# Queries and keys of twelve attention groups: a dense load, one split and a trip through DRAM in place of a threefold load and four splits

## Chip, core and metric

The kernel runs on one core of a Trainium2 chip. The metric is the device time of one execution in microseconds (us): the median over runs. Beside it stands one profiled execution, whose trace gives every row below. Its span is the time from its first to its last instruction.

## What is computed

Three layers in a row, all in float32: a gated linear attention over 4 batches, 8 heads, 768 positions and head dimension 40 (a recurrence with a forget gate, an input gate and an output gate), then a first feed-forward layer (320 to 768 to 320, the maximum of three projections), then a second one (320 to 2048 to 320, with h * relu6(h + 3) / 6).

```python
for t in range(S):                                   # attention
    m_new = np.maximum(f_gate[:, :, t] + m, i_gate[:, :, t])
    f_stab = np.exp(f_gate[:, :, t] + m - m_new); i_stab = np.exp(i_gate[:, :, t] - m_new); m = m_new
    C = f_stab * C + i_stab * outer(vt, kt);  n = f_stab * n + i_stab * kt
    y[:, :, t] = sigmoid(o_gate) * (C @ qt) / max(|n . qt|, 1)
h = np.maximum(np.maximum(x @ w1, x @ w2), x @ w3);  x = h @ w_out
h = x @ w_in;  out = (h * np.clip(h + 3, 0, 6) / 6) @ w_out
```

## The kernel before

The attention is cut into chunks of 128 positions: 6 chunks times 4 batches make 24 groups, numbered 0 to 23 in the code (the first one is group 0), each with all 8 heads. A group loads its queries and keys (`lq`, line 443), its keys, values and output gates in rows of positions (`lk`, line 454) and, from group 4 on, the forget factors (`fl`, line 504). VectorE scans the decays (`scan`, line 510); TensorE makes the scores (`sc`, line 538), the part from the earlier state (`inter`, line 566), the values' product (`pv`, line 608), the change of the state (`dc`) and a transpose of the result (`tr`); GpSimd, VectorE and ScalarE do what lies between. The first feed-forward layer (`f_in`, `f_out`, lines 789 and 822; its matmuls are those of lines 300, 833 and 835) works on blocks of groups, `BLK1` = 2, 2, 4, 4, 4, 4, 4, and is interleaved with the attention of later groups. The second layer follows (lines 953 to 1050); its start overlaps with the end of the first.

TensorE multiplies float32 in one pass when its operands are rounded (type F32R). Groups from 8 (`GF`) on therefore use a high part and a low part, and three products stacked along 120 partitions: rows 0 to 39 hold high times high, rows 40 to 79 and 80 to 119 one high and one low part. Before the change each of the groups 8 to 23 gets there so: `lq` loads q and k each three times, with six transfers of 40 x 1024 elements, into two `raw` buffers of 120 partitions; then, for q and k (`a`) and both halves of the heads (`z`), ScalarE writes the part to be taken away (`hm`, line 471: a copy scaled by 0 or 1 of each partition, from `lows`), and VectorE (q) or GpSimd (k) subtracts it (`ls`, line 476) into `qs`, the operand of the scores. `raw` and `qs` have two buffers, `sp` has one.

The order of all of this first part is made by a planner, not by hand: `Plan.add` (line 143) takes each step with its engine, an assumed duration, a priority and the tags that it reads and writes; `Plan.order` (line 160) simulates five in-order engines (SP issues the transfers), a clock of TensorE and the free buffers of `BUFS`, and takes whatever can start first, the lower priority number deciding ties. `MOVED` is a list of offsets to single steps' priorities. The result is a fixed order on each engine; on the chip each engine takes its instructions strictly in that order. The steps of the weights of the first layer (`weights`, line 747) load each tile into a ring of four buffers `wr` of 128 x 3072 bytes (`load_f64`, line 262); the second layer's weights use the same ring later (line 965).

Of the kernel before, what the change touches and what calls it, by code (L numbers as in the profile page):

```python
# [9 lines left out]
F32 = mybir.dt.float32  # L10
F32R = mybir.dt.float32r
# [5 lines left out]
ALU = mybir.AluOpType  # L17
# [3 lines left out]
B, H, S, D = 4, 8, 768, 40  # L21
L = 128
NC_ = S // L
G = B * NC_
# [3 lines left out]
K1, K2 = FF1 // 128, FF2 // 128  # L28
DP = 42
NBC, GF, G3 = 4, 8, 8  # L30
WC, OC = 384, 320
BLK1 = [2, 2, 4, 4, 4, 4, 4]
JOIN, LAG1 = 4, 3
# [2 lines left out]
AHEAD, WP0, WPR = 6, 500, 100  # L36
GP, NSG = 1055, 4
GPB, GGB = 3, 4
WLP, QLP = 800, 4000
PE_, PM, PC = 0, 2 * 10**6, 3 * 10**6  # L40

MOVED = {
# [20 lines left out]
}  # L63
NM1, NM2 = max(BLK1) * L, max(BLK2) * L

BUFS = dict(
    qs=2, raw=2, sp=1, kvo=2, kvg=2, fd=2, vt=2, vw=2, nm=2, rr=2, y=2, sg=2, ct=1, cn=B, ch=1, cs=B,
    pr=1, vr=1, wr=4, wa=2, x1=2, m=2, hh=3, x2=1, pa=3, h=2, acc0=1, acc1=1, acc2=1,
)
# [6 lines left out]
def top(x):  # L76
    return x.bitcast(BF16).rearrange("p h (t two) -> p h t two", two=2)[..., 1]


def low(x):  # L80
    return x.bitcast(BF16).rearrange("p h (t two) -> p h t two", two=2)[..., 0]
# [160 lines left out]
def body(tc, ctx, qk0, qkf, kvo, ig, fg, w1, w2, out):  # L242
    nc = tc.nc
# [4 lines left out]
    stg = ctx.enter_context(pool("stg"))  # L248
    dram = ctx.enter_context(pool("dram", 1, space=DRAM))
    psh = ctx.enter_context(pool("psh", 1, space=PSUM))  # L250
    psa = ctx.enter_context(pool("psa", 3, space=PSUM))

    f0_d = dram.tile([NC_ - 1, BH, L], F32, name="f0_d")
    x2_d = [dram.tile([128, 3, n * L], F32, name=f"x2_d{j}") for j, n in enumerate(BLK2)]

    def prio(p):
# [49 lines left out]
    with ExitStack() as c1:  # L306
# [5 lines left out]
        def sb(tag, g, shape, dt=F32, p=None):  # L312
            return (p or at).tile(shape, dt, tag=tag, name=f"{tag}{g}", bufs=BUFS[tag])
# [8 lines left out]
        lows = cs1.tile([120, 2], F32, name="lows")  # L322
        dL = cs1.tile([128, NC_ - 1, BH // 2], F32, name="dL")
        P = Plan()
# [3 lines left out]
        def gates(gp1, c0, c1_, pr):  # L328
# [96 lines left out]
            if c0:  # L425
# [2 lines left out]
                P.add("PE", 250, pr + 1500, dl1, r=[("dls",), ("own",)], w=[("pa", "dlp")])  # L428
                P.add("ACT", 230, pr + 1500, dl2, r=[("pa", "dlp")], w=[("dL",)])

        def attention(g):
            c, b = divmod(g, B)
            pr = 1000 * g
            j = next(j for j, (a, e) in enumerate(SP1) if a <= g < e)
            gi = g - SP1[j][0]
            s = T[g] = {}
            keep = c < NC_ - 1
            per_head = lambda x: x.unsqueeze(2).to_broadcast([128, H, DP])
            QS, FD, KVO = [("qs", g, a, z) for z in range(2) for a in range(2)], [("fd", g, a) for a in range(2)], ("kvg" if g < 2 else "kvo", g)
# [3 lines left out]
            def lq(a=0):  # L443
                if g < GF:
                    s["qs"] = sb("qs", g, [128, 2, 4, L])
                    for r in range(2):
                        nc.sync.dma_start(s["qs"][64 * r:64 * r + D], qk0[g][r])
                else:

                    s["raw", a] = q = sb("raw", f"{g}_{a}", [120, H, L])  # L450
                    for r in range(3):
                        nc.sync.dma_start(q[r * D:r * D + D].rearrange("p h t -> p (h t)"), qkf[g - GF, :, a])
# [8 lines left out]

            if g < GF:
                P.add("SP", 680, pr - 2100, lq, w=QS, size=4 * 40 * 2048)
            else:
                for a in range(2):
                    P.add("SP", 1100, pr - QLP + 400 * a, lambda a=a: lq(a), r=[("pv", g - AHEAD)], w=[("raw", (g, a))], size=120 * 4096)
            P.add("SP", 360, pr - 2000, lk, w=[KVO], size=4 * 128 * 976)

            if g >= GF:

                def hm(a, z):
                    s["sp", a, z] = sb("sp", f"{g}_{a}{z}", [120, 4, L], F32R)
                    x = s["raw", a][:, 4 * z:4 * z + 4]
                    nc.scalar.activation(s["sp", a, z], x, AF.Copy, scale=lows[:, a:a + 1])  # L474

                def ls(a, z):
                    if "qs" not in s:
                        s["qs"] = sb("qs", g, [120, 2, H, L], F32R)
                    x = slice(4 * z, 4 * z + 4)
                    eng = nc.gpsimd if a else nc.vector  # L480
                    eng.tensor_tensor(out=s["qs"][:, a, x], in0=s["raw", a][:, x], in1=s["sp", a, z].bitcast(F32), op=ALU.subtract)  # L481

                for z in range(2):
                    for a in range(2):
                        SPL, Q = ("sp", (g, a, z)), ("qs", g, a, z)
                        P.add("ACT", 600, pr - QLP + 1000 + z, lambda a=a, z=z: hm(a, z), r=[("raw", (g, a)), ("lows",)], w=[SPL])
                        P.add("POOL" if a else "DVE", 1220 if a else 600, pr - QLP + 1000 + z, lambda a=a, z=z: ls(a, z), r=[("raw", (g, a)), SPL], w=[Q])

            def fds():
                s["fd"] = sb("fd", g, [128, H, L])  # L490
# [106 lines left out]
            def pr0(a):  # L597
                if "pr" not in s:
                    s["pr"] = sb("pr", g, [128, H, L])
                x = slice(a * 4, a * 4 + 4)  # L600
                nc.vector.tensor_tensor(out=s["pr"][:, x], in0=s["fd"][:, x], in1=top(s["fd"])[:, x], op=ALU.subtract)

            def pr1(a):
                x = slice(a * 4, a * 4 + 4)
                eng = nc.vector if a else nc.gpsimd
                eng.tensor_tensor(out=low(s["pr"])[:, x], in0=s["pr"][:, x], in1=top(s["pr"])[:, x], op=ALU.subtract)
# [15 lines left out]
            if g >= G3:  # L622
                VR, PR = ("vr", g), [("pr", g, a) for a in range(2)]
                P.add("POOL", 800, pr + 31, vr0, r=[("vt", g)], w=[VR])
                P.add("POOL", 800, pr + 32, vr1, w=[VR])
                for a in range(2):
                    P.add("DVE", 830, pr + 33 + a, lambda a=a: pr0(a), r=[FD[a]], w=[PR[a]])
                    P.add("DVE" if a else "POOL", 1000 if a else 1310, pr + 36 + a, lambda a=a: pr1(a), w=[PR[a]])
                more = [VR, *PR]
            P.add("PE", 1290 if more else 1890, pr + 40, pv, r=[*FD, ("vt", g), *more], w=[PV, ("pv", g)], wait=300)  # L630

# [247 lines left out]
        def ids():  # L879
# [16 lines left out]
                out=sel, in0=ident[0:2 * BH, 0:BH], in1=ident[0:2 * BH, BH:2 * BH], op=ALU.add  # L896
# [187 lines left out]
def build(arrays):  # L1084
    nc = bacc.Bacc("TRN2", target_bir_lowering=False, num_devices=1)
    args = {
        n: nc.dram_tensor(f"in_{n}", a.shape, mybir.dt.from_np(a.dtype), kind="ExternalInput").ap()
        for n, a in arrays.items()
    }
    out = nc.dram_tensor("out_0", (B * S, DM), F32, kind="ExternalOutput").ap()  # L1090
    with tile.TileContext(nc, schedule_with_timeline_sim=True) as tc, ExitStack() as ctx:
        body(tc, ctx, out=out, **args)
    return nc
# [9 lines left out]
```

## Time and profile before

| | us |
|---|---|
| median of three runs | 798.19 |
| the three runs | 796.95, 799.6, 798.19 |
| the profiled execution | 794.38 |
| its span | 792.7 |
| TensorE busy in the span | 758.5 (96%) |
| GpSimd busy | 462.4 (58%) |
| VectorE busy | 437.4 (55%) |
| ScalarE busy | 353.3 (45%) |

PE is TensorE, PEld its weight loads, DVE VectorE, ACT ScalarE, POOL GpSimd, SP the engine that issues the transfers; a "q" behind the name means the sequencer of that engine. Busy shares are means over stages with different limits, so the rows below go by stretches of the span. A matmul's end is modelled, and a busy TensorE can still hold small gaps.

### The profile page before, as it was taken

What the parts mean: (1) busy time and instruction counts of PE and PEld (TensorE: products, weight loads), DVE (VectorE), ACT (ScalarE), POOL (GpSimd) and SP (SyncE); (2) the same over time, 40 slices, a digit from 0 to 9 for tenths busy, and PEclk for the clock granted to TensorE, in tenths of its full rate; (3) what the DMA queues carried; (4) which work ended last, traced back from release to release, by engine and by line L of the source; (5) the groups of instructions that cost most, each with busy time, mean ns of one, the idle gap of its engine ahead of it and who ended that gap; (6) DMA issues with size and microseconds to landing.
All of it is one profiled execution on the core that took longest, in us unless ns stands there. A gap on an engine that the chain in (4) does not pass through costs nothing.

```text
span 792.7 us, 13185 instructions
## 1 busy us (share of the span) xinstructions
PE 758.5 (96%) x5081; PEld 653.8 (82%) x5081; DVE 437.4 (55%) x652; ACT 353.3 (45%) x677; POOL 462.4 (58%) x420
## 2 busy tenths in 40 slices
PE   8899899899899999999899999999999999999997
PEld 5599898777777878778688888898999889898986
DVE  6868979889889888886414665313122113121210
ACT  4667633333334335332415887534433334433432
POOL 4568878998898887675512556544335334343332
PEclk9569989999999999999999999999999999999999
DMA  8578645344344435420502652100100000000000
GB/s 268 172 198 275 217 130 172 108 133 142 118 138 162 154 116 165 115 70 34 153 17 70 189 174 73 67 1 6 62 1 1 33 1 1 34 1 1 34 0 34
DMA packets 28654, 76.05 MB, mean 96 GB/s; under 512 B 3920, under 2 KB 9136, under 8 KB 28592
## 3 DMA queue, kind: packets, MB, share of 16 engines
q1 hardware_dynamic: 28592, 75.22, 30.1%
q8 instruction: 40, 0.66, 0.3%
q14 instruction: 22, 0.18, 0.1%
HBM read 65.54 MB, written 7.95 MB: 93 GB/s over the span
## 4 chain that ended last, share of the span: by engine, by line
PE 59%; DVE 13%; POOL 12%; ACT 7%; issue 5%; DMA 3%; SPq 0%; POOLq 0%; DVEq 0%; ACTq 0%
PE pi L300 20%; PE h L300 12%; PE po L1025 6%; PE po L1024 6%; PE po L1026 6%; POOL qs L481 3%; PE acc L833 3%; DVE fd L514 2%; DVE t L283 2%; POOL hh L817 2%; DVE qs L481 2%; POOL cs L730 1%; ACT a L271 1%; PE sc L544 1%; POOL y L655 1%
## 5 line engine op out<-in xcount | busy, mean ns | idle before, releaser
L1010 POOL TENSOR_TENSOR gg<-r,gg 128x512 fp32r<-128x512 f32 x96 | 125.7, 1318 | 183.2 <-ACT gg L1009 173.1
L300 PE MATMUL h<-x,w 128*128 128x512 f32 (+1 forms) x1008 | 227.2, 374 | 5.4 <-ACT m L801 4.2
L300 PEld LDWEIGHTS h<-x,w 128*128 128x128 f32 x1008 | 172.7, 195 | 36.3 <-ACT m L801 6.3
L300 PE MATMUL pi<-xs,w 128*128 128x512 f32 x768 | 193.5, 395 | 2.5 <-ACT w L969 1.9
L1007 DVE SCALAR_TENSOR_TENSOR r<-r,pi 128x512 f32<-128x512 f32 x96 | 64.3, 687 | 229.3 <-ACT r L1006 229.0
L300 PEld LDWEIGHTS pi<-xs,w 128*128 128x128 f32 x768 | 140.7, 188 | 31.0 <-ACT w L969 2.6
L1006 ACT ACTIVATE r<-pi,b 128x512 f32<-128x512 f32 x96 | 63.9, 686 | 133.8 <-PE pi L300 133.2
L1024 PE MATMUL po<-w,gg 128*128 128x320 f32 x384 | 118.2, 310 | 0.6 <-ACT x L861 0.4
L1025 PE MATMUL po<-w,gg 128*128 128x320 f32 x384 | 117.9, 309 | 0.0
L1026 PE MATMUL po<-w,gg 128*128 128x320 f32 x384 | 111.1, 309 | 0.0
L817 POOL TENSOR_TENSOR hh<-m,hh 128x512 fp32r<-128x512 f32 (+1 forms) x42 | 56.6, 1347 | 39.1 <-ACT hh L813 39.0
L1024 PEld LDWEIGHTS po<-w,gg 128*128 128x128 f32 x384 | 72.1, 188 | 4.8 <-ACT x L861 0.7
L1009 ACT CAST gg<-r 128x512 fp32r<-128x512 f32 x96 | 58.9, 621 | 36.5 <-DVE r L1007 34.4
L1025 PEld LDWEIGHTS po<-w,gg 128*128 128x128 f32 x384 | 72.1, 188 | 3.1
L474 ACT ACTIVATE sp<-raw,lows 120x512 fp32r<-120x512 f32 x64 | 46.3, 724 | 62.7 <-POOL qs L481 35.2
L833 PE MATMUL acc<-hh,w 128*128 128x512 f32 (+1 forms) x252 | 74.1, 374 | 0.0
L803 DVE TENSOR_TENSOR m<-h,m 128x512 f32<-128x512 f32 (+1 forms) x84 | 50.7, 603 | 42.3 <-PE h L300 36.5
L1026 PEld LDWEIGHTS po<-w,gg 128*128 128x128 f32 x384 | 70.4, 188 | 0.8
L514 DVE TENSOR_TENSOR_SCAN fd<-fd,ident 128x512 f32<-128x512 f32 x40 | 66.1, 1661 | 2.2 <-DMA fd<-f_d 2.2
L290 POOL TENSOR_TENSOR w<-t,w 128x384 fp32r<-128x384 f32 (+2 forms) x46 | 46.3, 1015 | 26.8 <-ACT w L768 16.8
L481 POOL TENSOR_TENSOR qs<-raw,sp 120x512 fp32r<-120x512 f32 x32 | 49.1, 1534 | 12.9 <-ACT sp L474 10.9
L813 ACT CAST hh<-m 128x512 fp32r<-128x512 f32 (+1 forms) x42 | 23.4, 558 | 70.8 <-PE acc L833 66.0
(109 smaller groups left out, 1082.4 us busy)
## 6 DMA issues: line engine op xcount, KB each, us to landing
raw<-in_qkf SPq DMA_DIRECT2D x96, 160.0 KB
raw<-in_w SPq DMA_DIRECT2D x34, 384.0 KB
kvo<-in_kvo SPq DMA_DIRECT2D x22, 488.0 KB
fd<-f_d SPq DMA_DIRECT2D x20, 512.0 KB
raw<-in_w SPq DMA_DIRECT2D x22, 320.0 KB
out<-ob SPq DMA_DIRECT2D x24, 160.0 KB
xr<-x_d SPq DMA_DIRECT2D x6, 512.0 KB
qs<-in_qk SPq DMA_DIRECT2D x16, 160.0 KB
```

What stands on the lines that cost most here:

```text
L300: nc.tensor.matmul(ps, wt[:, a:a + 128], x[:, r], start=n == 0, stop=n == len(order) - 1)
L481: eng.tensor_tensor(out=s["qs"][:, a, x], in0=s["raw", a][:, x], in1=s["sp", a, z].bitcast(F32), op=ALU.subtract)
L514: nc.vector.tensor_tensor_scan(out=half, data0=s.get(("bc", a), half), data1=ident4.rearrange("p h t -> p (h t)"), initial=0.0, op0=ALU.mu ...
L817: nc.gpsimd.tensor_tensor(out=t[:, 1], in0=T["m", j, k], in1=t[:, 0].bitcast(F32), op=ALU.subtract)
L833: nc.tensor.matmul(acc[a], wo[:, a * 128:128 + a * 128], h, start=first, stop=last)
L1006: nc.scalar.activation(r, ps, AF.Relu, bias=b3)
L1007: nc.vector.scalar_tensor_tensor(out=r, in0=r, scalar=6.0, in1=ps, op0=ALU.min, op1=ALU.mult)
L1009: nc.scalar.copy(gg[:, 0], r)
L1010: nc.gpsimd.tensor_tensor(out=gg[:, 1], in0=r, in1=gg[:, 0].bitcast(F32), op=ALU.subtract)
L1024: nc.tensor.matmul(po[t], hi, wo[:, 0:320], start=first, stop=False)
L1025: nc.tensor.matmul(po[t], hi, wo[:, 320:640], start=False, stop=False)
L1026: nc.tensor.matmul(po[t], lo, wo[:, 0:320], start=False, stop=last)
```

## The change

Groups 8 to 11 stay as they were. Groups 12 (`GH`) to 23 get their operand in another way. One transfer brings q and k once, cut densely into 128 partitions of 640 elements, into a buffer of the ring `wr`. ScalarE copies all of it, rounded, to a second buffer of the ring (the high part); GpSimd subtracts that from the first into a third (the low part). Two transfers write both parts to a DRAM buffer of the group, and five transfers read from there into the 120 partitions of `qs`. The planner's assumed durations of the old split and of two VectorE steps of the values' product are raised, and `MOVED` is another list, so the order of the whole first part is new. Nothing else is changed.

```diff
+GH = 12
+QF = 2 * D * H * L // 128
...
 MOVED = {
...
+    qs_d = [dram.tile([2, D, 2, H * L], F32, name=f"qs_d{g}") for g in range(GH, G)]
...
+        flat = lambda x: x.rearrange("d a n -> (d a n)").rearrange("(p f) -> p f", f=QF)
...
+                elif g >= GH:
+                    s["raw"] = stg.tile([128, QF], F32, tag="wr", name=f"qraw{g}", bufs=BUFS["wr"])
+                    nc.sync.dma_start(s["raw"], flat(qkf[g - GF]))
...
+            elif g >= GH:
+                P.add("SP", 380, pr - 4000, lq, r=[("pv", g - AHEAD)], w=[("wr", (100 + g, 2))], size=4 * 128 * QF)
...
+            if g >= GH:
+                d = qs_d[g - GH]
+                def part(n):
+                    s["sp", n] = stg.tile([128, QF], F32R, tag="wr", name=f"q{n}{g}", bufs=BUFS["wr"])
+                    return s["sp", n]
+                def sq():
+                    nc.scalar.copy(part(0), s["raw"])
+                def sl():
+                    nc.gpsimd.tensor_tensor(out=part(1), in0=s["raw"], in1=s["sp", 0].bitcast(F32), op=ALU.subtract)
+                def sw(n):
+                    nc.sync.dma_start(flat(d[n]), s["sp", n].bitcast(F32))
+                def sr():
+                    s["qs"] = q = sb("qs", g, [120, 2, H, L], F32R)
+                    q = q.bitcast(F32).rearrange("p a h t -> p a (h t)")
+                    nc.sync.dma_start(q[0:D], d[0])
+                    for r, (zq, zk) in enumerate(((0, 1), (1, 0)), 1):
+                        nc.sync.dma_start(q[r * D:r * D + D, 0], d[zq, :, 0])
+                        nc.sync.dma_start(q[r * D:r * D + D, 1], d[zk, :, 1])
+                QR, QP = ("wr", (100 + g, 2)), [("wr", (100 + g, n)) for n in range(2)]
+                P.add("ACT", 760, pr - 3000, sq, r=[QR], w=[QP[0]])
+                P.add("POOL", 1650, pr - 3000, sl, r=[QR, QP[0]], w=[QP[1]])
+                for n in range(2):
+                    P.add("SP", 360, pr - 3000 + n, lambda n=n: sw(n), r=[QP[n]], w=[("qd", g, n)], size=4 * 128 * QF)
+                P.add("SP", 1720, pr - 2500, sr, r=[("qd", g, 0), ("qd", g, 1)], w=QS, size=120 * 8192)
+            elif g >= GF:
...
-                        P.add("ACT", 600, pr - QLP + 1000 + z, lambda a=a, z=z: hm(a, z), r=[("raw", (g, a)), ("lows",)], w=[SPL])
-                        P.add("POOL" if a else "DVE", 1220 if a else 600, pr - QLP + 1000 + z, lambda a=a, z=z: ls(a, z), r=[("raw", (g, a)), SPL], w=[Q])
+                        P.add("ACT", 720, pr - QLP + 1000 + z, lambda a=a, z=z: hm(a, z), r=[("raw", (g, a)), ("lows",)], w=[SPL])
+                        P.add("POOL" if a else "DVE", 1320 if a else 850, pr - QLP + 1000 + z, lambda a=a, z=z: ls(a, z), r=[("raw", (g, a)), SPL], w=[Q])
...
-                    P.add("DVE", 830, pr + 33 + a, lambda a=a: pr0(a), r=[FD[a]], w=[PR[a]])
-                    P.add("DVE" if a else "POOL", 1000 if a else 1310, pr + 36 + a, lambda a=a: pr1(a), w=[PR[a]])
+                    P.add("DVE", 980, pr + 33 + a, lambda a=a: pr0(a), r=[FD[a]], w=[PR[a]])
+                    P.add("DVE" if a else "POOL", 1100 if a else 1310, pr + 36 + a, lambda a=a: pr1(a), w=[PR[a]])
```

## Rows read from the trace of the kernel before

**Rows 1.** Scores of line 544 from 170 to 360 us: durations, first and last start.

```profile
L544 PE MATMUL sc<-qs x96: 223/275/331, 176.3 to 356.0; 120*128 120x128 f32 x96
```

**Rows 2.** Stretches: length, each engine's busy time (instructions), clock, DMA share, GB/s.

```profile
core 0: us, PE busy (x) PEld busy (x) DVE busy (x) ACT busy (x) POOL busy (x), PEclk, DMA share, GB/s
0.00:120.00 120.00, 110.48 (x893) 95.32 (x894) 93.23 (x168) 70.62 (x161) 83.16 (x102) 0.84 0.68 210
120.00:170.00 50.00, 45.39 (x413) 38.49 (x413) 43.65 (x64) 17.27 (x34) 45.00 (x43) 0.97 0.43 136
170.00:360.00 190.00, 179.41 (x1451) 147.22 (x1450) 167.63 (x234) 74.55 (x138) 155.48 (x142) 1.00 0.41 129
360.00:400.00 40.00, 37.74 (x251) 30.44 (x250) 18.44 (x31) 12.77 (x22) 19.32 (x15) 1.00 0.33 101
400.00:520.00 120.00, 118.03 (x596) 101.36 (x596) 58.04 (x81) 73.75 (x151) 57.18 (x44) 1.00 0.29 95
520.00:760.00 240.00, 240.00 (x1328) 216.04 (x1327) 51.76 (x69) 93.91 (x154) 93.29 (x69) 1.00 0.04 15
```

**Rows 3.** TensorE's waits from 170 to 360 us: total, times, longest, in us.

```profile
PE sc L544 <- POOL qs L481: 5.8, 4, 2.0
PE h L300 <- ACT m L801: 1.8, 3, 0.7
PE dc L694 <- DVE x L675: 0.6, 1, 0.6
PE in L575 <- DVE qs L481: 0.6, 1, 0.6
PE tr L664 <- POOL y L655: 0.6, 1, 0.6
PE sc L544 <- DVE qs L481: 0.5, 1, 0.5
```

**Rows 4.** Groups by shape, 170 to 360 us: busy us, mean ns, idle before.

```profile
L481 POOL TENSOR_TENSOR qs<-raw,sp 120x512 fp32r<-120x512 f32 x23 | 36.8, 1602 | 9.2 <-ACT sp L474 7.5 <-issue 1.4
L474 ACT ACTIVATE sp<-raw,lows 120x512 fp32r<-120x512 f32 x46 | 33.3, 724 | 45.9 <-POOL qs L481 23.3 <-DVE qs L481 14.0 <-DMA raw<-in_qkf 7.7
L817 POOL TENSOR_TENSOR hh<-m,hh 128x512 fp32r<-128x512 f32 x18 | 26.8, 1487 | 9.2 <-ACT hh L813 9.2
L481 DVE TENSOR_TENSOR qs<-raw,sp 120x512 fp32r<-120x512 f32 x24 | 21.2, 884 | 6.3 <-ACT sp L474 6.1
L813 ACT CAST hh<-m 128x512 fp32r<-128x512 f32 x18 | 11.2, 620 | 33.1 <-PE acc L833 32.5 <-DVE m L803 0.5
```

**Rows 5.** Groups by shape, 520 to 760 us: the same kinds of steps, two widths.

```profile
L1010 POOL TENSOR_TENSOR gg<-r,gg 128x512 fp32r<-128x512 f32 x66 | 86.2, 1314 | 142.6 <-ACT gg L1009 140.6 <-PE po L1026 2.0
L985 POOL TENSOR_TENSOR xs<-xr,xs 128x1024 fp32r<-128x1024 f32 x3 | 7.2, 2408 | 4.6 <-ACT xs L984 4.6
L984 ACT CAST xs<-xr 128x1024 fp32r<-128x1024 f32 x3 | 3.1, 1037 | 0.0
```

**Rows 6.** Line 452 on SP, 170 to 360 us: duration of one issue, min/median/max ns.

```profile
L452 SPq DMA_DIRECT2D raw<-in_qkf x66: 281/324/522, 175.9 to 345.7; - x66
```

**Rows 7.** SP's own waits, 170 to 360 us: total, times, longest, in us.

```profile
SPq L452 <- POOL qs L481: 29.8, 11, 6.0
SPq L506 <- PE pv L618: 23.1, 9, 6.4
SPq L736 <- ACT ch L721: 19.3, 5, 6.1
SPq L456 <- PE dc L694: 18.3, 6, 6.2
```

**Rows 8.** The chain that ended last: start, duration in us, and what.

```profile
85.40 6.01 DMA cs<-ch
...
305.73 4.19 DMA x_d<-x
...
323.21 3.64 DMA raw<-in_qkf
```

**Rows 9.** VectorE's waits, 170 to 360 us.

```profile
DVE fd L514 <- DMA fd<-f_d: 2.2, 3, 1.1
```

**Rows 10.** One stretch, columns as in the second group.

```profile
40.00:80.00 40.00, 39.06 (x343) 36.86 (x343) 29.95 (x54) 26.79 (x62) 29.54 (x34) 0.85 0.78 233
```

**Rows 11.** Weight loads of line 264 on SP near the start of the second layer.

```profile
392.63 4.11 SPq L264 DMA_DIRECT2D raw<-in_w  x2
```

**Rows 12.** VectorE and GpSimd, line 481, 170 to 360 us: duration min/median/max ns.

```profile
L481 DVE TENSOR_TENSOR qs<-raw,sp x24: 673/755/1503, 171.7 to 352.7; 120x512 fp32r<-120x512 f32 x24
L481 POOL TENSOR_TENSOR qs<-raw,sp x23: 1268/1297/2317, 173.6 to 354.3; 120x512 fp32r<-120x512 f32 x23
```

More of the change, by code (lines that the diff above doesn't have):

```diff
@@ L467, in attention @@
             P.add("SP", 360, pr - 2000, lk, w=[KVO], size=4 * 128 * 976)
-            if g >= GF:
+            if g >= GH:
[23 more added lines that the diff above has]
+            elif g >= GF:
                 def hm(a, z):
```

34 rows, old and new, of the table MOVED are left out of this document.

## The prediction, made before the change was run

> **What bounds the kernel now.** First: where in time does the change act? The scores of the twelve groups 12 to 23 (eight matmuls each, 96 in all) run from 176.3 to 356.0 us [rows 1], so the stretch to look at is 170 to 360 us, 15.8 us for each group. The table by stretches comes next [rows 2]. From 520 to 760 us TensorE is busy all of the 240 us: the second layer runs at its own pace and nothing of the change can shorten it. From 170 to 360 us TensorE is busy for 179.4 of 190 us, VectorE for 167.6 (88%), GpSimd for 155.5 (82%), ScalarE for 74.6 (39%), and the transfers take 41% of their engines. So TensorE is the bound here too, with 10.6 us of idle time, and two other engines are close behind it. TensorE's work is not touched by the change: what can be won is idle time of TensorE, and only that. Around the stretch it idles 4.6 us (120 to 170), 2.3 us (360 to 400) and 2.0 us (400 to 520).
>
> The third view says what ended that idle time [rows 3]: 5.8 us the scores waited for GpSimd's `qs`, in four waits of up to 2.0 us; 0.5 us the scores and 0.6 us line 575 waited for VectorE's `qs`. These 6.9 us of 10.6 hang on the split that the change takes out. The other rows there (`m`, `x`, `y`) add 3.0 us. TensorE takes its instructions in a fixed order, so while a score waits for its operand, the feed-forward matmuls queued behind it wait too, ready as they are; that is why such a wait costs the end of the kernel.
>
> **The change, part by part.** Taken out, for each of the twelve groups [rows 4]: four ScalarE steps of 0.724 us, 2.90 us; two VectorE steps of 0.884, 1.77 us; two GpSimd steps of 1.602, 3.20 us. Added: one ScalarE copy of 640 elements and one GpSimd subtraction of 640. No row has that width, but 512 and 1024 elements stand there: ScalarE 0.620 [rows 4] and 1.037 us [rows 5], which gives 0.72 us at 640; GpSimd 1.314 and 2.408 us in the quiet second layer [rows 5], which gives 1.59 us, and since its 512 wide step takes 1.487 us in our stretch [rows 4], 1.13 times as long, 1.80 us here. Net, over twelve groups: ScalarE -26 us, VectorE -21 us, GpSimd -17 us. VectorE would be busy for 146 of 190 us (77%) and GpSimd for 139 (73%).
>
> These savings lie beside TensorE and are worth nothing by themselves. What they do is end the 6.9 us of waits for `qs`: the new operand is split well ahead and comes by a transfer. Term one: -6.9 us. Term two: the other waits of 3.0 us become shorter when VectorE and GpSimd are less full; the bounds are 0 and -3.7 (all that is left of the 10.6), and I take a third of the waits, -1.0 us, because these steps hang on the matmuls in front of them as much as on their engine.
>
> Against this stand new waits. SP issues eight transfers in place of six, 0.32 us each [rows 6]: 2.6 in place of 1.9 us of each 15.8, hidden as long as SP has free time. It has: it stood 90 us of the stretch in its four longest kinds of waits alone [rows 7], waiting for buffers. But it also gets waits of a new kind: the writes wait for ScalarE and GpSimd, and the reads wait until both writes have landed. Landings in the chain took 3.64 us (a load of q or k), 4.19 us (a store to DRAM) and 6.01 us (the copies of line 736) [rows 8]. One group's new way is a load (3.64), a copy (0.72), a subtraction (1.80), a write (4.19), five issues (1.6) and a read (3.64): 15.6 us, with 0.65 us for the issues of the writes 16.2 us, about one group's interval. The plan may begin a load after `pv` of six groups before, and the read needs only the `qs` buffer of the group two before it, so over a whole interval is left for the last 5.2 us. The nearest row is `fd`, which takes the same road today (SP, a transfer, two buffers): VectorE waited for it three times, 2.2 us in all [rows 9]. If TensorE waits for the new `qs` as rarely, it is 0 to 2.2 us; if each group's score waited as long as the longest does now, 12 x 2.0 = 24 us. I take 1.1 us, near the `fd` row, and keep the upper end for a rival.
>
> A rule of the Trainium skill speaks against this road: "DMA: Bandwidth & Descriptors", section "Two DMAs through the same engine are not ordered", says that a transfer that reads what another wrote must wait for the other's completion, which is what SP does here. Its section "Anatomy of one DMA" gives, for transfers issued by GpSimd, about 2 us fixed plus the bytes at 436 GB/s; 327,680 bytes would by that be an estimated 2.75 us. The row of this trace has 4.19 us for a store of 512 and 128 KB, issued by SP and beside other traffic. By the page a group's way would be about 1.4 us shorter and the new waits nearer to 0; I go by the row.
>
> Bytes: q and k of a group are 983,040 bytes today and 327,680 + 655,360 + 983,040 after it, another 0.98 MB, 11.8 MB in all. The stretch moves 129 GB/s now [rows 2], 24.5 MB; it would move 36.3 MB, 191 GB/s, a DMA share of some 0.6 by the same ratio. From 40 to 80 us the kernel ran at 233 GB/s and a share of 0.78 with TensorE busy for 39.06 of 40 us [rows 10]. Bandwidth is no bound; landings can grow somewhat.
>
> The ring `wr` is free: the second layer's weights are first loaded at 392.6 us [rows 11], after the last score. `qs`, the scores and all other steps keep their shape. The new order also moves steps before 170 us, which the trace can't price: TensorE idles 9.5 us of the first 120 and its clock is granted at 0.84 there [rows 2], between the levels 1.2 and 2.4 GHz. I take 0, with 3 us either way. Raised durations in the plan cost nothing by themselves.
>
> Does the gain last to the end? After 400 us TensorE is busy for 118 of 120 us, then without a gap [rows 2]: what arrives earlier is worked off earlier. If the second layer's weights, first loaded at 392.6 us [rows 11], did not come forward with it, the 2.0 us of idle time there would grow by up to the whole gain; that case stands in the rival in which nothing is left.
>
> Sum: -6.9 - 1.0 + 1.1 = -6.8 us. On the profiled execution (794.38 us, span 792.7 and 1.7 us around it) that is 787.6; it ran 3.8 us under the median of 798.19. On the median: 791.4 us.
>
> **The rivals.** *The whole gap closes.* If lighter engines keep every step ahead of TensorE, all its idle time from 120 to 400 us (4.6 + 10.6 + 2.3 = 17.5 us) goes: 780.7 us. For it: VectorE's `qs` steps took from 0.673 to 1.503 us for one shape, GpSimd's from 1.268 to 2.317 [rows 12], so these two delay each other, and 48 such steps become 12. Against it: 3.7 of the 10.6 us were waits for other things. The Trainium skill ("SBUF", section "Who interferes with whom") gives the reason: a VectorE step with two SBUF inputs and a GpSimd step that reads SBUF share a port that one of them holds alone. The spread just told agrees; by that rule the remaining steps of both speed up as well, towards the 780.7 us.
>
> *Nothing is left.* TensorE's fixed order meets the next late step instead: a score that no longer waits for `qs` waits for `fd`, or the transposes wait for `y`, or the weights of the second layer are late. Of 10.6 us idle the same 10 return: 796 to 800 us, taken as 798.2. For it: three engines at 82% and more leave many candidates. Against it: after the change VectorE and GpSimd are at three quarters.
>
> *Slower: SP holds up the operands.* SP is in order. While it waits for a landing of 4.19 us, or for GpSimd's subtraction, the `fd`, `kvo` and `cs` transfers behind it wait too; `fd` late makes the scan late, the scan the score. If each group's score waits 1.45 us (the mean of today's four waits, 5.8/4), it is 12 x 1.45 = 17.4 against the 7.9 won: +9.5, 807.7 us. It decides from 0.66 us a group (7.9/12). For it: SP's waits of up to 6.4 us [rows 7] show plan and chip drifting apart by more than a landing. Against it: the lead of over an interval.
>
> *It doesn't do what it says* would need the old split to stay for groups 12 to 23; the code leaves it for groups 8 to 11 alone, so no chance is given.
>
> **How the numbers follow.** Forecast (791.4, from 788 to 795) 0.47; whole gap (around 781 to 787) 0.15; nothing left 0.18; slower 0.20. A measurement of this kernel can tell about 0.3%, 2.4 us, from no change: faster 0.62, same 0.18, slower 0.20. For 8 in 10 the range takes in the rival of the whole gap nearly to its end, 782, and the lower half of the slower one, to 804: what is left out is about 0.07 below and 0.10 above.
>
> **What would show it.** Right: in the stretch of groups 12 to 23 no TensorE wait on line 481, GpSimd and VectorE near 73 to 77%, waits of the scores for the transfer of `qs` under 2.2 us in all, TensorE's idle time near 4 us of the stretch, and scores of group 23 some 6 us earlier. Wrong: scores that end their wait with a `qs` transfer or with `fd`, landings above 6 us, long SP waits on writes that have not landed, or a gain that the stretch shows and 400 to 520 us gives back. A change of the same size before 170 us would be the new order's, not the split's.

## The result, and the profile after

The changed kernel takes 788.39 us (median of 4 runs, 786.64 to 791.34) against 797.63 us of the kernel before (median of 4): a ratio of 0.9892, 95% interval 0.9861 to 0.9923. The forecast was 791.4, range 782 to 804. The profiled execution took 788.16 us (span 786.5), 6.2 us less than the profiled one of before; that one lay 3.3 us under its median, so the traces account for 6.2 us and not for all of the 9.2 between the medians.

The stretches of the changed kernel (columns as in [rows 2]), and the scores of the groups 12 to 23:

```profile
core 0: us, PE busy (x) PEld busy (x) DVE busy (x) ACT busy (x) POOL busy (x), PEclk, DMA share, GB/s
0.00:120.00 120.00, 111.82 (x912) 96.83 (x913) 94.59 (x172) 68.88 (x158) 87.03 (x104) 0.84 0.67 217
120.00:170.00 50.00, 46.61 (x414) 40.57 (x413) 39.34 (x59) 19.08 (x39) 44.52 (x45) 0.97 0.47 154
170.00:360.00 190.00, 183.75 (x1513) 152.55 (x1513) 140.70 (x221) 49.72 (x103) 133.27 (x132) 0.98 0.60 182
360.00:400.00 40.00, 36.88 (x206) 29.82 (x205) 15.14 (x22) 12.61 (x22) 15.40 (x11) 1.00 0.33 101
400.00:520.00 120.00, 118.03 (x603) 101.85 (x602) 58.05 (x81) 73.44 (x150) 57.15 (x44) 1.00 0.29 95
...
L579 PE MATMUL sc<-qs x96: 223/275/415, 172.5 to 346.0; 120*128 120x128 f32 x96
```

Beside [rows 2]: from 170 to 360 us TensorE's idle time fell from 10.6 to 6.3 us, before 170 us from 14.1 to 11.6, and from 360 to 400 us it grew from 2.3 to 3.1. VectorE is busy for 26.9 us less in the stretch, GpSimd for 22.2, ScalarE for 24.8. The last of the scores came at 346.0 us, 10 us earlier than in [rows 1]. From 400 us on nothing differs: the gain is kept.

What ended TensorE's idle time in the stretch now (total, times, longest), beside [rows 3]:

```profile
PE h L297 <- ACT m L836: 2.7, 3, 1.2
PE in L610 <- DVE cn L748: 2.4, 1, 2.4
PE dc L729 <- POOL vw L568: 0.7, 1, 0.7
PE tr L699 <- POOL y L690: 0.3, 1, 0.3
PE sc L579 <- DMA qs<-qs_d: 0.2, 1, 0.2
```

The 6.9 us of waits for `qs` have become 0.2 us for its transfer. Other waits took up part of the place: 6.1 us, against 3.0 in [rows 3] and 0.3 in one more row of the kernel before:

```profile
PE pv L618 <- DVE pr L606: 0.3, 1, 0.3
```

Three VectorE steps that the change does not touch, first before and then after it (170 to 360 us; busy, mean ns, idle before), and then the new GpSimd step (the eight of the stretch, and all twelve with min/median/max ns and first and last start):

```profile
L514 DVE TENSOR_TENSOR_SCAN fd<-fd,ident 128x512 f32<-128x512 f32 x24 | 40.1, 1681 | 2.2 <-DMA fd<-f_d 2.2
L601 DVE TENSOR_TENSOR pr<-fd 128x512 f32<-128x512 f32 x22 | 24.8, 1131 | 0.5
L548 DVE TENSOR_TENSOR fd<-sc,fd 128x512 f32<-128x512 f32 x24 | 16.2, 679 | 0.6 <-POOL vw L533 0.6
```

```profile
L549 DVE TENSOR_TENSOR_SCAN fd<-fd,ident 128x512 f32<-128x512 f32 x24 | 34.8, 1459 | 0.2 <-DMA fd<-f_d 0.2
L636 DVE TENSOR_TENSOR pr<-fd 128x512 f32<-128x512 f32 x26 | 21.7, 835 | 6.4 <-PE pv L653 3.2 <-POOL cs L765 2.6
L583 DVE TENSOR_TENSOR fd<-sc,fd 128x512 f32<-128x512 f32 x24 | 16.3, 681 | 8.2 <-POOL vw L568 7.6 <-PE sc L579 0.6
...
L485 POOL TENSOR_TENSOR q<-qraw,q 128x640 fp32r<-128x640 f32 x8 | 18.1, 2266 | 2.1 <-DMA qs_d<-q 1.4 <-ACT q L482 0.5
...
L485 POOL TENSOR_TENSOR q<-qraw,q x12: 1548/2004/3937, 100.1 to 277.8; 128x640 fp32r<-128x640 f32 x12
```

The same scan takes 1.46 in place of 1.68 us and the same subtraction 0.84 in place of 1.13: steps of VectorE with two operands in SBUF (the on-chip memory that holds `fd` and `pr`) ran faster in the changed kernel, where GpSimd has less to do. The third step reads one operand, the scores, from the memory that TensorE writes to (PSUM), and only the other from SBUF: it takes 0.68 us in both kernels.

The twelve new GpSimd steps start from 100.1 to 277.8 us and the scores of their groups from 172.5 to 346.0 us, so a group is split some 70 us before its scores.

### The profile page after: what moved, and what is told of

The parts are those of the page before. It is cut to its first block, busy times and chain, and to the rows that moved or that the text cites. A ratio compares the mean times of both kernels' runs of the same rounds, so it can differ in the third digit from the quotient of the medians.

```text
span 786.5 us, 13102 instructions
## 1 busy us (share of the span) xinstructions
PE 758.3 (96%) x5088; PEld 657.0 (84%) x5088; DVE 403.5 (51%) x628; ACT 327.0 (42%) x641; POOL 438.3 (56%) x408
## 4 chain that ended last, share of the span: by engine, by line
PE 66%; POOL 12%; ACT 7%; DMA 6%; DVE 6%; issue 3%; SPq 1%; POOLq 0%; ACTq 0%; DVEq 0%
PE pi L297 20%; PE h L297 15%; PE po L1060 6%; PE po L1059 6%; PE po L1061 6%; PE acc L868 4%; DVE t L280 2%; DMA qs<-qs_d 2%; POOL hh L852 2%; PE sc L579 2%; DMA raw<-in_w 2%; POOL w L287 2%; POOL cs L765 2%; PE pv L653 1%; ACT a L268 1%
## 5 line engine op out<-in xcount | busy, mean ns | idle before, releaser
L297 PEld LDWEIGHTS pi<-xs,w 128*128 128x128 f32 x768 | 140.7, 188 | 29.7 <-ACT w L1004 1.2
L1041 ACT ACTIVATE r<-pi,b 128x512 f32<-128x512 f32 x96 | 63.8, 685 | 134.0 <-PE pi L297 133.3
L549 DVE TENSOR_TENSOR_SCAN fd<-fd,ident 128x512 f32<-128x512 f32 x40 | 60.0, 1506 | 0.3 <-DMA fd<-f_d 0.2
L868 PEld LDWEIGHTS acc<-hh,w 128*128 128x128 f32 x252 | 45.6, 192 | 7.1
L280 DVE SCALAR_TENSOR_TENSOR t<-a,t 128x384 uint32<-128x384 uint32 (+1 forms) x56 | 41.3, 753 | 17.6 <-ACT t L276 17.3
```

The source lines that it names most:

```text
L297: nc.tensor.matmul(ps, wt[:, a:a + 128], x[:, r], start=n == 0, stop=n == len(order) - 1)
L549: nc.vector.tensor_tensor_scan(out=half, data0=s.get(("bc", a), half), data1=ident4.rearrange("p h t -> p (h t)"), initial=0.0, op0=ALU.mu ...
L868: nc.tensor.matmul(acc[a], wo[:, a * 128:128 + a * 128], h, start=first, stop=last)
L1041: nc.scalar.activation(r, ps, AF.Relu, bias=b3)
```

## Experiments

Three theories. A: the gain is the operand, which TensorE no longer waits for. B: it is the new order of all steps. C: it is the freed time of VectorE and GpSimd, whoever waits for them. And the rival of the prediction that would have made it slower: SP, standing for landings, holds up the operands. The code cuts are shortened: `...` and the comments stand for lines left out. Ratios are to the kernel before in runs on the same chip, with 95% intervals; the medians of before were 799.83, 795.58 and 796.40 us in the three batches.

### The new road in the old order, and the old road in the new one

`new_path_old_order`: `MOVED` and the planned durations of before, with the steps of group g+1 in the places of group g's loads and splits.

```diff
-        s["raw", a] = ...three loads...      # group g, a = 0
+        qload(g + 1)                         # one dense load
...
-        nc.scalar.activation(s["sp", a, z], x, AF.Copy, scale=lows[:, a:a + 1])
+        qhigh(g + 1)                         # at the third of the four
...
-        eng.tensor_tensor(out=s["qs"][:, a, x], ...)
+        qlow(g + 1)                          # next GpSimd place; both writes; the reads 10 steps behind the last
```

> The fixed order of the kernel before is kept for every step that both kernels have, with its planned durations; groups 12 to 23 get their operand by the dense load, the one split and the trip through DRAM, placed where the old loads and splits of the group in front of them stood, one group's interval early. Theory A (the gain is the operand: TensorE no longer waits for the split): 790 to 793 us. Theory B (the gain is the new order of all steps, the road of the operand hardly counts): 796 to 800 us. Rival (SP and the landings hold up the operands unless the order is made for them): over 800 us.

Measured: 788.28 us, ratio 0.9866 (0.9805 to 0.9926), no different from the changed kernel's 0.9892 and a little below the 790 to 793 us of theory A. The road of the operand brings the gain in the old order too; the new `MOVED` list is not needed for it. Theory B falls.

`old_path_new_order`: the order of the changed kernel, with the threefold load and the four splits.

```diff
 def sr():
-    nc.sync.dma_start(q[0:D], d[0])          # and four more reads
+    for k, (z, i) in enumerate(((0, 0), (0, 1), (1, 0), (1, 1))):
+        pend.append((T["n"] + 5 * k, g, lambda z=z, i=i: piece(z, i)))   # a ScalarE copy, a VectorE or GpSimd subtraction
```

> The fixed order of the changed kernel is kept, but groups 12 to 23 load threefold again and are split by four ScalarE, two VectorE and two GpSimd steps, placed where the changed kernel reads the operand from DRAM, spread over some 15 steps. Theory A: 795 to 800 us, with TensorE waiting for the split again. Theory B: 788 to 791 us.

Measured: 815.16 us, ratio 1.0212 (1.0160 to 1.0263): 2% slower than before, and outside what either theory expected. TensorE did not wait for the split, as theory A had it, but for other steps (170 to 360 us):

```profile
PE tr L719 <- POOL y L710: 7.1, 3, 4.1
PE h L297 <- ACT m L856: 5.4, 5, 2.2
PE pv L673 <- DVE fd L603: 2.7, 1, 2.7
PE dc L749 <- POOL vw L586: 2.2, 1, 2.2
```

No row names the split's result, so a split's cost can show in the waits for other steps of the same engines. That is the first mark against the strict form of A. The places of the four splits are mine, bunched within some 15 steps, so the size of the loss is not that of the split in a planned place.

### The engines filled again, with nobody waiting

`load_back` adds constant work to the changed kernel, three ScalarE copies, two VectorE and one GpSimd subtraction a group; `load_dve`, `load_pool` and `load_act` add one engine's share alone (two, one and three steps).

```diff
+def again(k):
+    t = sb("sp", f"{g}_{k}", [120, 4, L], F32R)
+    nc.scalar.activation(t, ident4[0:120], AF.Copy, scale=lows[:, 0:1])
+    u = sb("raw", f"{g}_{k}", [120, H, L])
+    eng = nc.gpsimd if k == 1 else nc.vector
+    eng.tensor_tensor(out=u[:, 0:4], in0=ident4[0:120], in1=t.bitcast(F32), op=ALU.subtract)
...
 def sr():
+    for k in range(3):
+        pend.append((T["n"] + 5 * k, g, lambda k=k: again(k)))
```

> The changed kernel, and in each of the groups 12 to 23 three ScalarE copies, two VectorE and one GpSimd subtraction of 120x512 elements more, on constants, which nobody waits for: the engines are as full as before the change, but the scores do not wait for them. Theory A, strict form (only the wait for the operand counted): 788 to 790 us. Theory C (the freed time of VectorE and GpSimd carries the gain): 794 to 798 us.

Measured: 807.29 us, 1.0128 (1.0064 to 1.0193). No score waits for these steps, and yet the whole gain is lost and more. Theory A in its strict form falls; C holds, with a larger price than the 794 to 798 us expected. The three pairs of steps share one `sp` buffer, and ScalarE stood 31 us of the stretch for the subtractions that free it:

```profile
ACT sp L493 <- DVE raw L496: 16.4, 10, 3.6
ACT sp L493 <- POOL raw L496: 14.6, 10, 3.0
```

> The changed kernel, and in each of the groups 12 to 23 two VectorE subtractions of 120x512 elements on constants in SBUF more, which nobody waits for: what the old split took of VectorE, 21 us in all. If VectorE's freed time carries the gain: 796 to 800 us. If GpSimd's does: 788 to 791 us. If both count: 792 to 796 us.

Measured: 795.13 us, 0.9987 (0.9956 to 1.0018).

> The changed kernel, and in each of the groups 12 to 23 one GpSimd subtraction of 120x512 elements on constants more: about what the change freed on GpSimd, 18 us in all. If GpSimd's freed time carries the gain: 794 to 800 us. If VectorE's does: 788 to 791 us. If both count: 791 to 796 us.

Measured: 793.44 us, 0.9973 (0.9936 to 1.0009).

> The changed kernel, and in each of the groups 12 to 23 three ScalarE copies of 120x512 elements on constants more: what the change freed on ScalarE, 26 us in all. ScalarE is busy for a quarter of the stretch, so every theory of the busy engines gives 788 to 791 us; if it is the copies of the feed-forward layer on ScalarE that come late behind any other step, 793 to 798 us.

Measured: 788.34 us, 0.9908 (0.9875 to 0.9941).

VectorE's share alone takes the gain back, GpSimd's alone nearly so, ScalarE's leaves it. Both medians lie where their expectations have "both count". Put back one at a time, the two cost 0.0079 and 0.0065 against `load_act` in the same batch, together more than the 0.0108 of the gain: they are not shares that add up. The added steps stand at one place each, from the reads of the operand on and some five steps apart; no run puts them elsewhere, so how much of the loss is the work and how much its place is open. The stretch from 170 to 360 us of `load_dve` and then of `load_pool`:

```profile
170.00:360.00 190.00, 179.22 (x1496) 148.10 (x1496) 159.08 (x236) 49.16 (x101) 140.52 (x128) 0.99 0.61 182
```

```profile
170.00:360.00 190.00, 182.71 (x1512) 151.35 (x1512) 145.17 (x223) 49.95 (x102) 148.07 (x142) 0.98 0.61 182
```

Work on VectorE alone (159.1 for 140.7 us) also raises GpSimd's busy time, from 133.3 to 140.5 us for four steps fewer in the window, and work on GpSimd alone (148.1 us) raises VectorE's to 145.2: by these rows each slows the other.

`dve_one` asks whether it is this mutual slowing or VectorE's own time.

```diff
-nc.vector.tensor_tensor(out=u[:, 0:4], in0=ident4[0:120], in1=ident4[0:120], op=ALU.subtract)
+nc.vector.tensor_reduce(u[:, 0, 0:4], ident4[0:120], axis=mybir.AxisListType.X, op=ALU.add)
```

> As load_dve, with two VectorE sums over one operand in SBUF (120x4x128 to 120x4) in each of the twelve groups in place of the two subtractions with two operands in SBUF, for about the same time on VectorE. If VectorE's queue alone counts: as load_dve, 0.997 to 1.000 of the kernel before. If it is that VectorE and GpSimd hold each other up: as the changed kernel, 0.989 to 0.992, and GpSimd's busy time in the stretch falls from load_dve's 140 us towards 133.

Measured: 791.28 us, 0.9928 (0.9898 to 0.9958). The added steps of `load_dve` and of `dve_one` (busy, mean ns), and a GpSimd step that neither touches, in the one and in the other:

```profile
L493 DVE TENSOR_TENSOR raw<-ident 120x512 f32<-120x512 f32 x22 | 23.1, 1052 | 0.0
...
L861 POOL TENSOR_TENSOR hh<-m,hh 128x512 fp32r<-128x512 f32 x17 | 28.2, 1660 | 14.9 <-ACT hh L857 14.8
```

```profile
L493 DVE TENSOR_REDUCE raw<-ident 120x4 f32<-120x512 f32 x22 | 14.6, 668 | 0.0
...
L861 POOL TENSOR_TENSOR hh<-m,hh 128x512 fp32r<-128x512 f32 x17 | 26.1, 1533 | 23.8 <-ACT hh L857 23.8
```

With one operand in SBUF the added step is not drawn out (0.67 for 1.05 us) and GpSimd is not either (its busy time in the stretch is 130.2 us). With the step that reads PSUM and kept its 0.68 us, this shows that a VectorE step with two SBUF operands and a GpSimd step hold each other up. The Trainium skill ("SBUF — State Buffer", section "Who interferes with whom") states that a VectorE instruction with two SBUF inputs contends with a GpSimd instruction that reads SBUF; these rows agree. For the time it is not decisive: the added steps also took 14.6 for 23.1 us, and the loss in proportion to that, 0.63 of 0.0095, gives 0.995, inside the interval.

### What is left of the split

`no_split` leaves out load, split and writes of groups 13 to 23, which read group 12's parts and so score with its queries and keys.

```diff
 def lq(a=0): ...    def sq(): ...    def sl(): ...    def sw(n): ...
+    if g > GH:
+        return
...
 def sr():
+    d = qs_d[0]
```

> The changed kernel without the load, the split and the writes of groups 13 to 23: their operand is read from group 12's buffer in DRAM, so they use the wrong queries and keys. Eleven ScalarE copies, eleven GpSimd subtractions and 33 transfers are left out. Theory A: 787 to 789 us, since what is left of the split lies beside TensorE. Theory C: 784 to 786 us, as GpSimd is freed of another 20 us. Rival (the round trip still costs): under 784 us.

Measured: 780.29 us, 0.9748 (0.9695 to 0.9802), where A gave 787 to 789 and C 784 to 786: it lies in the range of the expectation's third reading, that the round trip still costs (under 784). The stretch:

```profile
170.00:360.00 190.00, 189.20 (x1600) 157.72 (x1600) 138.91 (x228) 44.87 (x94) 119.53 (x127) 1.00 0.46 135
```

With GpSimd at 119.5 us and a third of the new road's transfers gone TensorE idles 0.8 us of 190, near the rival "the whole gap closes" with its 780.7 us. This run takes away GpSimd's step, ScalarE's and 33 transfers together, and with the ring `wr` free six weight loads of the second layer come at 105 to 113 us in place of 280 to 294 (the ring comes up again below). So it does not say which of them the 8 us below the changed kernel (11 by the ratios) belong to, and it does not bear out C alone.

`act_vt` moves another step of 0.95 us from GpSimd to ScalarE, in the changed kernel; `act_vt_old_order` does it in `new_path_old_order`.

```diff
+if g >= GH:
+    for h in range(H):
+        nc.scalar.activation(s["vt"][:, h], s["v"][:, h], AF.Copy, scale=isl[:, h:h + 1])
+    return
 nc.gpsimd.tensor_tensor(out=s["vt"], in0=s["v"], in1=per_head(isl), op=ALU.mult)
```

> The changed kernel with the gated values of groups 12 to 23 (line 561, one GpSimd step of 0.95 us) made by eight ScalarE steps of 42 elements each instead: frees GpSimd of some 11 us, and puts some 20 us on ScalarE. Theory C (GpSimd's time still limits the stretch): 782 to 786 us, 0.981 to 0.987 of the kernel before. Otherwise (the values come later, ScalarE's copies for the feed-forward layer too): 788 to 793 us.

Measured: 789.68 us, 0.9905 (0.9869 to 0.9941).

> new_path_old_order (the order of the kernel before, the new road of the operand) with the gated values of groups 12 to 23 made by ScalarE as in act_vt. Theory C: 0.978 to 0.985 of the kernel before. Otherwise: 0.986 to 0.992.

Measured: 790.61 us, 0.9933 (0.9896 to 0.9971). Neither gains; the fair measure for the second is `new_path_old_order`, 0.9866. GpSimd fell to 125.2 us in the stretch of `act_vt`, but eight steps take 1.9 us of ScalarE in place of one of 0.95 on GpSimd (20.6 us for 88 steps, which overlap: one by itself lasts 0.317), so the values come later, and ScalarE's next steps too:

```profile
L563 ACT ACTIVATE vt<-kvo,idt 128x42 f32<-128x42 f32 x88 | 20.6, 317 | 3.4 <-PE pv L657 2.1 <-DMA kvo<-in_kvo 1.3
```

C expected a gain from both and got none. Either GpSimd's busy time no longer limits after the change, or the later values cost as much as it gave; these runs do not tell the two apart. That filling the engines again costs the gain is shown, that freeing them further pays is not.

### SP and the landings

`hop` adds a second trip through DRAM in front of the reads.

```diff
 def sr():
+    e = qs_e[g - GH]
+    nc.sync.dma_start(flat(e[0]), flat(d[0]))
+    nc.sync.dma_start(flat(e[1]), flat(d[1]))
-    nc.sync.dma_start(q[0:D], d[0])
+    nc.sync.dma_start(q[0:D], e[0])          # and the other four from e
```

> The changed kernel with a second trip through DRAM: each part is copied from DRAM to another buffer in DRAM before the five reads, so in each of the twelve groups SP stands for one more landing of about 4 us, with the loads of the forget factors, keys and values queued behind it. If the lead of the operand is ample, as forecast: 788 to 792 us. If the rival is right that SP's waits hold up the operands: from 800 us on, about 1.2 us a group or more.

Measured: 816.06 us, 1.0234 (1.0174 to 1.0294): 27 us more than the changed kernel by the two ratios. SP's and then TensorE's waits in `hop` (120 to 400 us, and 120 to 420 us):

```profile
SPq L497 <- DMA qs_e<-qs_d: 44.3, 12, 6.8
```

```profile
PE h L298 <- ACT m L840: 11.1, 5, 3.5
PE sc L583 <- DMA qs<-qs_e: 10.2, 2, 6.6
PE in L614 <- DVE cn L752: 5.1, 1, 5.1
PE in L614 <- DMA qs<-qs_e: 4.3, 1, 4.3
```

SP stood 44.3 us for twelve landings, 3.7 us each, and the time grew by 2.3 us a group. TensorE waited 14.5 us for the operand itself. The rival is real. How much of the loss is SP's standing is not separated: the run also adds 24 transfers of 320 KB. In the changed kernel the reads never stood for the writes: what they waited for from 170 to 360 us was mainly the buffer `qs`:

```profile
SPq L493 <- PE in L610: 9.8, 1, 9.8
SPq L493 <- PE sc L579: 5.9, 4, 2.5
SPq L493 <- DMA qs<-qs_d: 0.9, 1, 0.9
```

### Two groups more

`gh10` starts the new road at group 10, in the order of before (`GH = 10` in `new_path_old_order`).

> new_path_old_order with the change from group 10 on, so for fourteen groups: another 8 ScalarE, 4 VectorE and 4 GpSimd steps are replaced by 2 and 2. Theory C: 1 to 2 us less than with twelve groups, 0.983 to 0.988 of the kernel before. If the landings limit it: 0.988 to 0.995.

Measured: 786.75 us, 0.9879 (0.9830 to 0.9928). It can't be told from the twelve groups (0.9866 in the same order, 0.9892 in the changed kernel), so the 1 to 2 us that C expected are neither seen nor ruled out. None of the runs that compute everything beats the changed kernel clear of the intervals.

## Why the prediction was right, and where it was not

- *The bound and the place of the gain*: right in the place, short in the size. TensorE's idle time in the stretch fell to 6.3 us, where about 4 was forecast, and nothing was given back from 400 us on.
- *Term one, -6.9 us for the waits for `qs`*: the waits went, to 0.2 us, but as a cause the term was half of the truth. "These savings lie beside TensorE and are worth nothing by themselves" is the sentence that failed: the same kind of work put back where nobody waits for it costs the whole gain (`load_dve`) or most of it (`load_pool`). A reading that fits, though no run shows it step by step: in TensorE's fixed order a wait that goes is partly replaced by another, and an engine with room catches up before the next step is late, so the row named `qs` because its steps were the last in a full queue.
- *Term two, -1.0 us for the other waits*: wrong in sign by the rows of the stretch, 3.3 us before and 6.1 after. `old_path_new_order`, with 17 us in its four longest rows, suggests that without the engines' freed time they would have grown further.
- *The engines' loads*: VectorE -21 forecast and -26.9 measured. The extra is the steps that are no longer drawn out, 0.22 us of each scan and 0.30 of each subtraction. The chance for this stood with the largest rival; it belonged to the sum. GpSimd's -17 was for all twelve new steps, and the -22.2 of the stretch holds only eight of them, four having run before 170 us; those eight took 2.27 us in the mean, not 1.80.
- *New waits, +1.1 us*: measured 0.2 us, with a lead far longer than the one interval that was counted (some 70 us from split to score). `hop` does not test that lead: its copies stand right in front of the reads, so SP stands for each of them, and that is the prediction's own rival. Landings were longer than the rows of before: writes and reads of the chain took

```profile
265.88 4.25 DMA qs<-qs_d
270.65 9.15 DMA qs_d<-q
280.28 5.02 DMA qs<-qs_d
328.36 6.84 DMA qs<-qs_d
```

  against the 3.64 and 4.19 of [rows 8] in the sum. The page of the Trainium skill that gave an estimate of 2.75 us, for a transfer issued by GpSimd ("DMA: Bandwidth & Descriptors", section "Anatomy of one DMA"), lay further off than the row.
- *"The ring `wr` is free"*: wrong. [rows 11] are not the first loads of the second layer's weights. The first layer has 24 weight tiles; the kernel before made 30 weight loads by 88.4 us, so six of the second layer's were among them (the last six, first line). In the changed kernel, where the new buffers come first in the ring, these six come at 279.8 to 294.3 us (second line), and SP stands 11.0 us there for writes to land (third line):

```profile
L264 SPq DMA_DIRECT2D raw<-in_w x6: 328/340/382, 74.4 to 88.4; - x6
L261 SPq DMA_DIRECT2D raw<-in_w x6: 327/330/357, 279.8 to 294.3; - x6
SPq L261 <- DMA qs_d<-q: 11.0, 3, 5.0
```

  So the changed kernel did stand for landings, and it cost TensorE something: behind the 9.15 us write the chain goes on (pieces of it below) to a weight load, ScalarE's work on it, VectorE and `in`, which is the 2.4 us wait for `cn`, the longest single wait of TensorE in the stretch:

```profile
279.82 0.36 SPq L261
285.32 8.10 DMA raw<-in_w
293.44 0.48 ACT a L268
294.74 0.68 DVE m L838
295.42 0.25 DVE cn L748
295.72 1.80 PE in L610 x8
```

- *Bytes*: 182 GB/s and a share of 0.60 measured, 191 and 0.6 forecast.
- *The new order, 0 with 3 us either way*: not contradicted. The old order with the new road is as fast. TensorE's idle time before 170 us fell by 2.5 us, which by the forecast's own test is the order's, but it is not clear of the spread: before 120 us the changed kernel idles 8.2 us, and `load_act` and `load_dve`, whose first added steps come after 150 us, idle 9.5 and 11.3 (first line `load_act`, second `load_dve`).

```profile
0.00:120.00 120.00, 110.51 (x889) 96.18 (x894) 92.59 (x169) 66.26 (x153) 84.37 (x103) 0.83 0.67 211
0.00:120.00 120.00, 108.69 (x929) 95.36 (x934) 95.75 (x174) 69.08 (x158) 88.58 (x105) 0.87 0.68 217
```

- *The rest of the 9.2 us*: the stretch gave 4.3, the time before 170 us 2.5, 360 to 400 us took 0.8 back, and 3.3 us lie between the profiled execution of before and its median; those no row explains. The -6.8 was forecast for the stretch alone, which gave less. That the median came within 3 us of 791.4 is in part luck: what the stretch lacked was made up by time that the forecast had put at 0 and by the profiled execution of before, which lay further below its median than that of after.

## What to carry to other kernels

A wait row names the step that came last, and taking that step away is worth what its engine then gets done earlier for everybody; so when several engines are over 80% busy, price the freed time of each engine and test it by putting the same work back where nobody needs it. A trip through DRAM could replace work on busy engines here at a profit, with the split some 70 us ahead of its use; `no_split` leaves open what the trip itself still costs. Ask of every buffer that such a trip borrows who else uses it, and where the issuing queue will stand for a landing: one more stand of 3.7 us in each group, with the transfers that came with it, cost three times what the change had won. A better order was not what made this change pay, but an order made for one road was poor for the other, with the old splits bunched as they were.

## What the runs showed of the hardware that was not expected

- VectorE steps with two operands in SBUF and GpSimd steps draw each other out by a good deal: 1.05 us for a 120x512 subtraction among GpSimd's steps against 0.67 us for a one-operand sum over the same elements, and 0.68 us before and after the change for a step with one operand in PSUM; a GpSimd step of 128x640 elements took between 1.5 and 3.9 us.
- A ScalarE step of only 42 elements a partition took 0.317 us, and eight of them, overlapping, 1.9 us: more than the one GpSimd step of 336 elements that they replaced (0.95 us).
- A write of 320 KB to DRAM took up to 9.15 us in the chain, in a stretch with a mean transfer share of 0.60.
